# A task graph with list-scheduled engines, uncast hardware-queue loads, and the attention matmuls of two heads side by side in an attention and feed-forward kernel

## The chip, the cores and the metric

The kernel runs on one core of a Trainium2 chip. The metric is the device time of one execution in microseconds (us), lower is better. A profile is one execution; its span is some 2 us shorter than the time.

## The reference, cut to what matters

```python
# q, k, v: (8 batches, 8 heads, 576 tokens, 64), float32
scores = q @ k.T / sqrt(64);  scores = where(|i - j| <= 32, scores, -1e9)
attn = softmax(scores);       x = (attn @ v) as (8*576, 8*64)
# feed-forward: w_in (512, 2048), w_out (2048, 512)
h = x @ w_in;  g = s * relu(h)**2 + b;  out = g @ w_out        # (4608, 512) float32
```

The feed-forward is 9 blocks of 512 tokens. A block has a first stage, s1 (16 groups of 4 matmuls of 512 columns), and a second, s2 (4 groups of 16): 1152 matmuls in all. A block needs the attention of the one or two batches whose tokens it holds.

## The kernel before

A hand-written interleaving: between the steps of a head's attention one feed-forward item or transpose is put in. The GpSimd (POOL) queue loads q, k and v and casts them to bf16 on the way; q is transposed by DMA, k on TensorE; each head has its own matmuls, and its sums come from 64 columns of ones next to v.

```python
# loads: cast by the software queue, 256 B in, 128 B out
op("pool", lambda e: e.dma_start(
      dst[0:ns, blk, :].rearrange("p (h d) -> p h d", h=H),          # bf16 tile
      src[b, :, s0:s0 + ns, :].rearrange("h s d -> s h d")), ...)    # float32 in DRAM
# q by DMA transpose, 128 x 128 at a time
op("sp", lambda e: e.dma_start(QT[slot][:, pr, s0:s0 + ns],
      QPRE[slot][0:ns, blk, pr * 128:(pr + 1) * 128], transpose=True), ...)
# scores of one head: 64 rows of the array
op("pe", lambda e: e.matmul(SC[bank][0:nk, col:col + nq],
      lhsT=KT[slot][hb:hb + 64, pr, key0:key0 + nk],
      rhs=QT[slot][hb:hb + 64, pr, q0:q0 + nq], start=True, stop=True), ...)
# weighted sum and row sums of one head: [v | ones], 128 columns
op("pe", lambda e: e.matmul(AVACC[:, coff + rc0:coff + rc0 + nn],
      lhsT=VT[slot][0:nk, wi, h, vcol0:vcol0 + 128], rhs=et[0:nk, ecol:ecol + nn], ...), ...)
# ... 1/sum = exp(-ln(sum)) on ScalarE over 64 partitions, then XT = AVACC * (1/sum) on VectorE
# ... order of all engines: do_fill() between the steps, by hand
```

The softmax here doesn't subtract the row's maximum and nothing guards it: scores larger than these inputs give would overflow.

Of the kernel before, what the change touches and what calls it, by code (L numbers as in the profile page):

```python
# [17 lines left out]
NSBLK = (S + 127) // 128  # L18
# [4 lines left out]
class _Tok:  # L23

    __slots__ = ("sem", "val", "seq", "used")

    def __init__(self, sem, seq, val=None):
        self.sem = sem
        self.seq = seq
        self.val = val  # L30
        self.used = False


class _Op:
    __slots__ = ("stream", "fn", "sig", "amount", "tok", "eager")

    def __init__(self, stream, fn, sig, amount, tok, eager):
        self.stream = stream
        self.fn = fn
        self.sig = sig  # L40
        self.amount = amount
        self.tok = tok
        self.eager = eager


class _Wait:
    __slots__ = ("stream", "toks")

    def __init__(self, stream, toks):
        self.stream = stream  # L50
        self.toks = toks


class _Raw:
    __slots__ = ("stream", "fn")

    def __init__(self, stream, fn):
        self.stream = stream
        self.fn = fn


class _Sched:

    STREAMS = ("pe", "act", "dve", "pool", "sp")

    def __init__(self, sems):
        self.sem = sems
        self.seqctr = {k: 0 for k in sems}
        self.cnt = {k: 0 for k in sems}
        self.items = []  # L70
        self.clock = {k: {} for k in self.STREAMS}
        self.last_writer = {}
        self.readers = {}

    def _need(self, req, tok):
        if tok is None:
            return
        cur = req.get(tok.sem)
        if cur is None or tok.seq > cur.seq:
            req[tok.sem] = tok  # L80

    def _emit_waits(self, stream, req):
        clk = self.clock[stream]
        needed = []
        for sname, tok in req.items():
            c = clk.get(sname)
            if c is not None and c.seq >= tok.seq:
                continue
            clk[sname] = tok
            tok.used = True  # L90
            needed.append(tok)
        if needed:
            self.items.append(_Wait(stream, needed))

    def op(self, stream, fn, reads=(), writes=(), waits=(), accum=False, group=None):
        req = {}
        for w in waits:
            self._need(req, w)
        for r in reads:
            self._need(req, self.last_writer.get(r))  # L100
        for w in writes:
            if not accum:
                self._need(req, self.last_writer.get(w))
                for tok in self.readers.get(w, {}).values():
                    self._need(req, tok)
        if stream == "pe":
            req.pop("pe", None)
        self._emit_waits(stream, req)

        if group is not None:  # L110
            sig_name = group.sem
            amount = 16
            tok = group.final
            eager = True
            self.cnt[sig_name] += 16
        else:
            sig_name = stream
            amount = 1
            self.seqctr[sig_name] += 1
            tok = _Tok(sig_name, self.seqctr[sig_name])  # L120
            eager = False

        for r in reads:
            self.readers.setdefault(r, {})
            self._need(self.readers[r], tok)
        for w in writes:
            self.last_writer[w] = tok
            if not accum:
                self.readers[w] = {}
        self.items.append(_Op(stream, fn, sig_name, amount, tok, eager))  # L130
        return tok

    def raw(self, stream, fn):
        self.items.append(_Raw(stream, fn))

    def wait(self, stream, waits):
        req = {}
        for w in waits:
            self._need(req, w)
        self._emit_waits(stream, req)  # L140

    def dma_group(self, stream, names, rot, ndma):
        i = rot.setdefault("i", 0)
        name = names[i % len(names)]
        rot["i"] = i + 1
        prev = self.cnt[name]
        if prev > 0:
            self.wait(stream, [_Tok(name, self.seqctr[name], prev)])
        self.seqctr[name] += 1
        final = _Tok(name, self.seqctr[name], prev + 16 * ndma)  # L150

        class _G:
            pass

        g = _G()
        g.sem = name
        g.final = final
        return g

    def finalize(self):  # L160
        counts = {k: 0 for k in self.sem}
        streams = {k: [] for k in self.STREAMS}
        sems = self.sem
        for it in self.items:
            if isinstance(it, _Raw):
                streams[it.stream].append(it.fn)
            elif isinstance(it, _Wait):
                toks = it.toks

                def runw(eng, toks=toks):  # L170
                    for t in toks:
                        assert t.val is not None, "wait on an unassigned token"
                        eng.wait_ge(sems[t.sem], t.val)

                streams[it.stream].append(runw)
            else:
                do_inc = it.eager or it.tok.used
                if it.eager:
                    counts[it.sig] += it.amount
                elif do_inc:  # L180
                    counts[it.sig] += it.amount
                    it.tok.val = counts[it.sig]
                fn = it.fn
                sig = it.sig
                amount = it.amount

                if do_inc:
                    def runo(eng, fn=fn, sig=sig, amount=amount):
                        ins = fn(eng)
                        ins.then_inc(sems[sig], amount)  # L190
                else:
                    def runo(eng, fn=fn):
                        fn(eng)

                streams[it.stream].append(runo)
        self.streams = streams
        self.cnt_final = counts


def bass_sliding_window_symmetric__then__act_starrelu_kernel(  # L200
# [12 lines left out]
    NBLK_M = (T + 511) // 512  # L213

    with ExitStack() as es:
        _uid = {"n": 0}

        def sb(shape, dt, nm="t"):
            _uid["n"] += 1
            return es.enter_context(nc.sbuf_tensor(f"{nm}_{_uid['n']}", list(shape), dt))  # L220

        def ps(shape, dt=F32, nm="ps"):
            _uid["n"] += 1
            return es.enter_context(nc.psum_tensor(f"{nm}_{_uid['n']}", list(shape), dt))
# [4 lines left out]
        QPRE = [sb((128, NSBLK, DM), BF16, "qpre") for _ in range(2)]  # L229
        KPRE = [sb((128, NSBLK, DM), BF16, "kpre") for _ in range(2)]  # L230
        VT = [sb((128, NSBLK, H, 192), BF16, "vt") for _ in range(2)]
        QT = [sb((128, NPAIR, S), BF16, "qt") for _ in range(2)]
        KT = [sb((128, NPAIR, S), BF16, "kt") for _ in range(2)]
        EA = [sb((128, 352), BF16, "ea") for _ in range(2)]
        EB = [sb((128, 480), BF16, "eb") for _ in range(2)]
        RLN = [sb((128, S), F32, "rln") for _ in range(2)]
        RREC = [sb((128, S), F32, "rrec") for _ in range(2)]
        MA = sb((128, 352), BF16, "ma")
        MB = sb((128, 480), BF16, "mb")
        ONES_BF = sb((128, 192), BF16, "onesb")  # L240
        IDENT = sb((128, 128), BF16, "ident")
        ZERO_F = sb((128, 1), F32, "zero")
        GT = [sb((128, 16, 512), BF16, "gt") for _ in range(2)]
        R1 = [sb((128, 512), BF16, "r1") for _ in range(4)]
        OUTS = [sb((128, 512), F32, "outs") for _ in range(2)]
        CVEC128 = sb((128, 512), F32, "cvec128")
        CVEC_ROW = sb((1, 512), F32, "cvecrow")
        SB128 = sb((128, 2), F32, "sb128")
        SB_ROW = sb((1, 2), F32, "sbrow")
        ONES_ROW_F = sb((1, 128), F32, "ones_row_f")  # L250
        BCOL_BF = sb((128, 1), BF16, "bcol")

        SC = [ps((128, 512), F32, "sc") for _ in range(2)]
        TP = ps((128, 8, 128), BF16, "tp")
        AVACC = ps((128, 1024), F32, "avacc")
        HT = [ps((128, 512), F32, "ht") for _ in range(2)]
        OUTP = [ps((128, 512), F32, "outp")]

        dmaP = [f"dmaP{i}" for i in range(10)]
        dmaO = [f"dmaO{i}" for i in range(6)]  # L260
        dmaT = [f"dmaT{i}" for i in range(4)]
# [448 lines left out]
        def fill(n_items: int, batches_done: int):  # L710
            done = 0
            while done < n_items:
# [14 lines left out]
                if not progressed:  # L727
                    break
# [96 lines left out]
```

## Time and profile before

439.0 us, median of 3 runs (438.4 to 440.4).

The page gives busy tenths in 40 equal slices of the 437 us span (a digit is 10.9 us; 9 is 90% or more).

```profile
PE   0465459948998999899989989989998999999986
ACT  1064648971688677788788868777777333444300
DMA  3999999919610991494099165100000101011012
```

The first ten slices are thin on TensorE (PE) while the DMA engines are full: the kernel waits for its loads. The queues on the page say with what (packets, MB, share of the time of 16 DMA engines):

```profile
q0 software_dynamic: 115168, 18.36, 58.2%
q1 hardware_dynamic: 25792, 13.59, 12.3%
```

110,592 of the first are the 256-byte pieces of q, k, v, 33 ns each on average. The busy time of the engines in stretches (stretch, its length, then busy us and count of instructions by engine, granted TensorE clock as a share of full speed, DMA share, GB/s; the DMA share adds up the times of all packets, so it passes 1 where packets overlap on an engine):

```profile
core 0: us, PE busy (x) PEld busy (x) DVE busy (x) ACT busy (x) POOL busy (x), PEclk, DMA share, GB/s
40.00:90.00 50.00, 35.74 (x228) 17.15 (x231) 22.59 (x52) 35.85 (x57) 15.06 (x19) 1.00 1.49 144
90.00:140.00 50.00, 42.14 (x255) 18.87 (x259) 23.19 (x49) 31.16 (x48) 12.58 (x15) 0.90 0.68 60
140.00:190.00 50.00, 44.96 (x308) 21.42 (x313) 26.93 (x60) 37.60 (x60) 20.47 (x25) 1.00 1.01 88
190.00:240.00 50.00, 47.09 (x316) 22.17 (x322) 27.73 (x62) 39.83 (x62) 17.28 (x21) 1.00 1.12 95
240.00:290.00 50.00, 47.63 (x307) 22.07 (x312) 28.54 (x62) 39.23 (x62) 4.21 (x5) 1.00 0.35 58
```

From about 140 us TensorE is busy 45 to 48 us of every 50. A piece of the timeline at 123 us (start, duration, engine, line of the kernel, instruction and its count) shows what attention costs there; sc are scores, avacc weighted sums, ht and outp the feed-forward:

```profile
123.08 0.49 PE L475 MATMUL sc<-qt,kt 64*128 64x192 bf16 x3
123.50 1.04 PE L581 MATMUL ht<-xt,win 128*128 128x512 bf16 x4
124.38 0.32 PE L533 MATMUL avacc<-ea,vt 128*128 128x160 bf16 x3
124.53 0.48 PE L533 MATMUL avacc<-eb,vt 128*128 128x64 bf16 x6
125.17 0.81 PE L581 MATMUL ht<-xt,win 128*128 128x512 bf16 x3 [0.16 <-issue]
125.91 0.32 PE L475 MATMUL sc<-qt,kt 64*128 64x160 bf16 x2
126.17 1.90 PE L635 MATMUL outp<-wout,gt 128*128 128x512 bf16 x8
```

By start-to-start times a head's scores take 0.26 + 0.42 us and its weighted sum 0.57 us, so a batch of 8 heads about 10 us. From 337 us only the feed-forward is left, at 216 ns a matmul (8 in 1.73 us).

| | before |
|---|---|
| time, us | 438.7 |
| TensorE / ScalarE / VectorE busy, us | 371 / 262 / 204 |
| first s1 matmul, us | 57 |
| attention of a batch on TensorE, start to start | 10 us, plus 1.4 us of k transposes |

### The profile page before, as it was taken

What the parts mean: (1) busy time and instruction counts of PE and PEld (TensorE: products, weight loads), DVE (VectorE), ACT (ScalarE), POOL (GpSimd) and SP (SyncE); (2) the same over time, 40 slices, a digit from 0 to 9 for tenths busy, and PEclk for the clock granted to TensorE, in tenths of its full rate; (3) what the DMA queues carried; (4) which work ended last, traced back from release to release, by engine and by line L of the source; (5) the groups of instructions that cost most, each with busy time, mean ns of one, the idle gap of its engine ahead of it and who ended that gap; (6) DMA issues with size and microseconds to landing.
All of it is one profiled execution on the core that took longest, in us unless ns stands there. A gap on an engine that the chain in (4) does not pass through costs nothing.

```text
span 437.0 us, 6159 instructions
## 1 busy us (share of the span) xinstructions
PE 371.2 (85%) x2208; PEld 172.9 (40%) x2248; DVE 204.4 (47%) x430; ACT 262.1 (60%) x401; POOL 107.8 (25%) x140
## 2 busy tenths in 40 slices
PE   0465459948998999899989989989998999999986
PEld 0234224322443444444444434444443444444432
DVE  7444325543555464565555555544554333334321
ACT  1064648971688677788788868777777333444300
POOL 8998092019000830380092030000000000000000
PEclk9999999987999999999999999999999999999999
DMA  3999999919610991494099165100000101011012
GB/s 21 142 146 196 182 174 153 78 19 146 54 48 32 102 109 54 57 150 80 26 120 114 57 74 51 59 26 24 25 26 24 50 24 48 25 48 46 27 49 74
DMA packets 140990, 32.34 MB, mean 74 GB/s; under 512 B 133792, under 2 KB 135840, under 8 KB 140960
## 3 DMA queue, kind: packets, MB, share of 16 engines
q0 software_dynamic: 115168, 18.36, 58.2%
q1 hardware_dynamic: 25792, 13.59, 12.3%
q8 instruction: 18, 0.29, 0.3%
q14 instruction: 12, 0.10, 0.1%
HBM read 36.70 MB, written 9.44 MB: 106 GB/s over the span
## 4 chain that ended last, share of the span: by engine, by line
PE 72%; ACT 8%; POOL 7%; DMA 6%; issue 4%; DVE 3%; DVEq 0%; POOLq 0%; ACTq 0%
PE ht L581 26%; PE outp L621 15%; PE outp L635 14%; PE sc L475 8%; DMA kpre<-in_k_dram 6%; PE avacc L533 6%; ACT rln L545 3%; POOL kpre L372 2%; ACT rrec L552 2%; PE tp L421 2%; POOL vt L400 2%; POOL qpre L372 2%; DVE xt L558 2%; PE outp L348 1%; DVE outs L644 1%
## 5 line engine op out<-in xcount | busy, mean ns | idle before, releaser
L581 PE MATMUL ht<-xt,win 128*128 128x512 bf16 x550 | 143.9, 389 | 7.8 <-DVE xt L558 4.5
L558 DVE TENSOR_TENSOR xt<-avacc,rrec 64x576 bf16<-64x576 f32 x64 | 48.3, 755 | 95.0 <-ACT rrec L552 89.2
L581 PEld LDWEIGHTS ht<-xt,win 128*128 128x128 bf16 x576 | 49.1, 99 | 59.8 <-issue 6.8
L400 POOL DMA_DIRECT2D vt<-in_v_dram x40 | 34.0, 899 | 151.1 <-PE avacc L533 123.1
L621 PE MATMUL outp<-wout,gt 128*128 128x512 bf16 x279 | 67.0, 380 | 4.2 <-DVE outs L644 2.5
L635 PE MATMUL outp<-wout,gt 128*128 128x512 bf16 x283 | 68.8, 385 | 0.6 <-issue 0.5
L545 ACT ACTIVATE rln<-avacc,zero 64x576 f32<-64x576 f32 x64 | 47.0, 734 | 30.9 <-PE avacc L533 30.0
L488 ACT ACTIVATE eb<-sc,zero 128x480 bf16<-128x480 f32 x64 | 42.3, 661 | 26.1 <-PE sc L475 26.1
L475 PE MATMUL sc<-qt,kt 64*128 64x192 bf16 (+2 forms) x320 | 54.9, 258 | 1.0 <-DVE kt L431 0.4
L488 ACT ACTIVATE ea<-sc,zero 128x352 bf16<-128x352 f32 x64 | 35.2, 550 | 27.0 <-PE sc L475 26.7
L552 ACT ACTIVATE rrec<-rln,zero 64x576 f32<-64x576 f32 x64 | 49.4, 772 | 2.1
L475 PEld LDWEIGHTS sc<-qt,kt 64*128 64x128 bf16 (+1 forms) x320 | 22.3, 100 | 54.1 <-issue 29.1
L591 ACT ACTIVATE r_32<-ht,zero 128x512 bf16<-128x512 f32 x36 | 24.8, 688 | 28.6 <-PE ht L581 27.5
L533 PE MATMUL avacc<-ea,vt 128*128 128x160 bf16 (+2 forms) x192 | 22.0, 228 | 23.2 <-DVE xt L558 22.9
L591 ACT ACTIVATE r_30<-ht,zero 128x512 bf16<-128x512 f32 x36 | 24.7, 687 | 27.5 <-PE ht L581 26.5
L621 PEld LDWEIGHTS outp<-wout,gt 128*128 128x128 bf16 x288 | 26.1, 98 | 36.0 <-DVE outs L644 4.5
L635 PEld LDWEIGHTS outp<-wout,gt 128*128 128x128 bf16 x288 | 26.8, 99 | 31.7 <-issue 1.3
L372 POOL DMA_DIRECT2D kpre<-in_k_dram x40 | 38.0, 950 | 0.0
L372 POOL DMA_DIRECT2D qpre<-in_q_dram x40 | 37.8, 944 | 0.7 <-issue 0.7
L644 DVE SCALAR_TENSOR_TENSOR outs<-outp,sb_37,cvec_35 128x512 f32<-128x512 f32 x36 | 26.9, 748 | 22.4 <-PE outp L635 22.2
L495 DVE TENSOR_TENSOR eb<-eb,mb 128x480 bf16<-128x480 bf16 x64 | 26.0, 406 | 18.9 <-ACT eb L488 16.4
L533 PE MATMUL avacc<-eb,vt 128*128 128x64 bf16 (+3 forms) x384 | 33.2, 209 | 0.0
(45 smaller groups left out, 252.0 us busy)
## 6 DMA issues: line engine op xcount, KB each, us to landing
out_dram<-outs SPq DMA_DIRECT2D x36, 256.0 KB, 2.0
qpre<-in_q_dram POOLq DMA_DIRECT2D x32, 128.0 KB, 5.3
kpre<-in_k_dram POOLq DMA_DIRECT2D x32, 128.0 KB, 5.4
vt<-in_v_dram POOLq DMA_DIRECT2D x32, 128.0 KB, 4.8
qt<-qpre SPq DMA_TRANSPOSE x140, 4.9
win<-in_moe_w_in_dram POOLq DMA_DIRECT2D x1, 2048.0 KB, 15.6
wout<-in_moe_w_out_dram POOLq DMA_DIRECT2D x1, 2048.0 KB, 26.8
qpre<-in_q_dram POOLq DMA_DIRECT2D x8, 64.0 KB, 6.5
```

The source lines that it names most:

```text
L372: lambda e, src=src, dst=dst, s0=s0, ns=ns, blk=blk: e.dma_start(dst[0:ns, blk, :].rearrange("p (h d) -> p h d", h=H), src[b, :, s0:s0 + n ...
L400: lambda e, s0=s0, ns=ns, blk=blk: e.dma_start(VT[slot][0:ns, blk, :, 64:128], v[b, :, s0:s0 + ns, :].rearrange("h s d -> s h d"),),
L475: lambda e, key0=key0, nk=nk, q0=q0, nq=nq, col=col: e.matmul(SC[bank][0:nk, col:col + nq], lhsT=KT[slot][hb:hb + 64, pr, key0:key0 + nk], ...
L488: lambda e, ncols=ncols, et=et, prows=prows: e.activation(et[0:prows, 0:ncols], SC[bank][0:prows, 0:ncols], AF.Exp, bias=ZERO_F[0:prows, : ...
L533: stop=stop, coff=coff: e.matmul(AVACC[:, coff + rc0:coff + rc0 + nn], lhsT=VT[slot][0:nk, wi, h, vcol0:vcol0 + 128], rhs=et[0:nk, ecol:ec ...
L545: lambda e: e.activation(RLN[hp][srow0:srow0 + 64, :].rearrange("p (g c) -> p g c", g=2), acc2(srow0), AF.Ln, bias=ZERO_F[srow0:srow0 + 64 ...
L552: lambda e: e.activation(RREC[hp][orow0:orow0 + 64, :], RLN[hp][srow0:srow0 + 64, :], AF.Exp, bias=ZERO_F[srow0:srow0 + 64, :], scale=-1.0,),
L558: lambda e: e.tensor_tensor(XT[orow0:orow0 + 64, pr, t0:t0 + S].rearrange("p (g c) -> p g c", g=2), acc2(orow0), RREC[hp][orow0:orow0 + 64 ...
L581: lambda e, kc=kc: e.matmul(HT[hbank][:, 0:nt], lhsT=WIN_BF[:, kc, ft * 128:(ft + 1) * 128], rhs=XT[:, kc, t0:t0 + nt], start=(kc == 0), s ...
L591: lambda e: e.activation(R1[rslot][:, 0:nt], HT[hbank][:, 0:nt], AF.Relu, bias=ZERO_F[:, :], scale=1.0,),
L621: lambda e, fc=fc, obuf=obuf: e.matmul(OUTP[obuf][0:nr, :], lhsT=GT[gslot][:, fc, sub * 128:sub * 128 + nr], rhs=WOUT_BF[:, fc, :], start= ...
L635: lambda e, fc=fc, obuf=obuf: e.matmul(OUTP[obuf][0:nr, :], lhsT=GT[gslot][:, fc, sub * 128:sub * 128 + nr], rhs=WOUT_BF[:, fc, :], start= ...
```

## The change

The intent: (1) let a list scheduler order each engine's instructions from a graph of tasks with estimated costs, in place of the hand-made order; (2) load float32 by the hardware queues, without the slow cast, and cast on VectorE; (3) treat two heads at once: their score matmuls on rows 0-63 and 64-127 of the array, their sums on columns 0-63 and 64-127, so that both softmax activations use 128 partitions. Further, q and k of batches 2 to 7 are transposed by DMA, 128x512 at a time. A unit is half of the queries (320 or 256) of a pair of heads; a batch has 8.

```diff
+    def plan(self):                      # list scheduling: always the task that can start first
+                for t in open_[s]:
+                    c = (max(free[s], t.ready), t.key, t.n)
+            free[t.stream] = st + t.cost
+            if t.dma is not None:
+                dma_free = max(dma_free, st + 1300.0) + t.dma[1]
+                t.fin = dma_free + 700.0
... (the order so found is what each engine's program is)
-                    op("pool", lambda e, ...: e.dma_start(dst[0:ns, blk, :]..., src[b, ...]...))
+                lambda e: e.dma_start(STG[n][0:ns, blk, :].rearrange("p (h d) -> p h d", h=H), ...),
+                650.0, writes=[("STG", n, blk)], key=16 * (b - 2), waits=waits,
+                dma=("l" if stream == "sp" else "a", ns * 2048 / 290.0))
+            return add("dve", lambda e: e.tensor_copy(dst[0:ns, lo:hi, :], STG[n][0:ns, lo:hi, :]),
+                       150 + 267.0 * len(blks), ...)
+            add("sp", lambda e: e.dma_start(dst[:, :, s0:s0 + ns], NAT[n][0:ns, blk, :],
+                                            transpose=True), 1300.0, ..., dma=("t", 700.0), ...)
+            for (w, q0, nq) in PIECES[hf]:
+                for hh in range(2):       # two heads: two row tiles
+                    ... e.matmul(SC[:, hh, c0:c0 + nq],
+                        lhsT=KT[slot][64 * hh:64 * hh + 64, pr, 128 * w:128 * w + 128],
+                        rhs=QT[slot][64 * hh:64 * hh + 64, pr, q0:q0 + nq], start=True, stop=True)
+            for (dst, res) in ((SS, "SS"), (AV, "AV")):   # row sums, then weighted sum
+                ... e.matmul(dst[64 * hh:64 * hh + 64, ...], lhsT=lhs,      # two column tiles
+                             rhs=EX[e_][:, hh, c0:c0 + nq], ...)
+                    for n in "qkv":
+                        load(b, n, blk, waits=[wout[3]] if b == 1 else ())  # after the weights
... (hand-made interleaving, phase_A_steps, phase_B, fill and drain_moe removed)
```

The tile for the float32 data (STG) has one copy, and each engine runs its program strictly in the planned order.

## The prediction

> **What bounds it now.** Three stages, from the busy table by stretches and the timeline.
> (1) 0-116 us, fill. TensorE is busy 71 of 116 us, and slowly: the clock record has it at full rate only from about 70 us, and the ht matmuls at 57-66 us lie about 430 ns apart instead of 216. The chain of waits shows why: the POOL queue issues loads (0.88 us each), then 26 us of one load of k in flight while both weight matrices share the DMA engines (90% and more in the slices from 11 to 77 us). A casting 256 B packet takes 32-35 ns; a batch of q, k, v is 13,824 of them, 28 us of all 16 engines.
> (2) 116-337 us: TensorE saturated, 206 of 221 us busy. By start-to-start times one head costs 1.25 us (scores 0.26 + 0.42, weighted sum 0.57), a transposed block of k 0.28, eight 512-column matmuls 1.73-1.83. ScalarE is busy 171, VectorE 119: not the limit.
> (3) 337-437 us: feed-forward alone, 216 ns a matmul, at its floor.
>
> **What the change does.** The 1152 feed-forward matmuls x 216 ns = 249 us stay: the floor.
> - Two heads per matmul: 36 matmuls a pair of heads instead of 28. The Trainium skill ("TensorEngine Tiling (Array Packing)", Tiling Modes and Performance Considerations) gives up to 2x, but a change of mode drains the array, and column tiling loses fast weight load; no run yet shows either. Estimate from the times above: 0.75-1.2 us for a unit (half the queries of a pair of heads), 6-9.6 us a batch where 10 us stood; plus 1.4 us a batch of k transposes gone. Steady gain: 2-5 us a batch.
> - ScalarE: both softmax activations now use 128 partitions, so about 262 -> 228 us. VectorE: -28 us by the same filling, +43 us of casts (estimate: fp32 copies at two elements a cycle, "VectorE: DVE Perf Modes", perf-mode tier table; no fp32 SBUF copy is in the trace). About 200 us, off the path.
> - Loads without cast, on hardware queues, by data rate: I expect 18-25 ns a 256 B packet (the transposes' SBUF packets average 24), so a batch in 16-22 us instead of 28. Weights only after the first nine blocks, batch 1 after the weights. First feed-forward block near 32 us (was 57), but batch 1 lands near 65, so its attention ends and s1(1) starts near 75-80 us, against about 116 for steady work before. This is the larger gain, some 35 us.
>
> **Sum.** 78 + 8 blocks x 27.6 + 6 batches x 6-9.6 + 4 of tail = 339-360; with 3-4% of stalls, 358 us. Range 330-402. Faster by over 2%: 0.93; within 2%: 0.03; slower: 0.04.
>
> **What would show it.** First ht matmul near 30-35 us; DMA slices full until about 65 us; k/q/v packets under 25 ns; TensorE 90% busy from 80 us to the end; score and sum groups 0.3-0.4 us each start to start; VectorE wait on TensorE, not the reverse.
>
> **What would make it wrong.** A transpose of 128x512 may hold the SP queue several times the 1.23 us of today's 128x128: 60 of them at over 3.5 us would make SP the limit (400-450 us). Loads may not get faster than 33 ns a packet (+15-25 us). The two heads may not overlap (+20 us). The fixed order may stall TensorE where ScalarE runs late (+10-20 us).

## The result, and the profile after

The changed kernel is correct and takes 401.3 us, median of 4 runs (399.1 to 402.7), beside 438.7 us (437.7 to 440.4). The ratio is 0.912 (95% interval 0.908 to 0.916). Ratios here are the mean time of one kernel's runs over that of the other's of the same rounds, so not quite the ratio of the medians. Executions over 1.5% slower than the fastest of the same kernel are left out of the means. It is faster, but the time lies at the very top of my range of 330 to 402 us, one of the four runs above it, and the gain is 37 us where I had forecast 81.

The slices (10.0 us each) and queues of the changed kernel:

```profile
PE   0636988892996897789796969999999999999996
ACT  1547662653595387457464737677777764433310
DMA  8999999849968978967999542310000010010112
```

```profile
q1 hardware_dynamic: 141536, 43.40, 54.0%
q0 software_dynamic: 4288, 4.20, 6.4%
```

The start is better filled, and a 256-byte packet now takes 22 ns, but from 90 to 240 us TensorE has holes that were not there before. The same stretches:

```profile
core 0: us, PE busy (x) PEld busy (x) DVE busy (x) ACT busy (x) POOL busy (x), PEclk, DMA share, GB/s
40.00:90.00 50.00, 45.16 (x324) 19.71 (x327) 30.15 (x70) 26.51 (x41) 0.00 (x0) 0.93 0.92 168
90.00:140.00 50.00, 36.95 (x267) 16.04 (x269) 24.85 (x51) 27.36 (x45) 0.00 (x0) 0.86 1.06 188
140.00:190.00 50.00, 44.16 (x332) 19.42 (x336) 27.30 (x60) 33.65 (x54) 0.00 (x0) 0.93 0.85 165
190.00:240.00 50.00, 38.60 (x282) 17.23 (x286) 25.65 (x54) 26.33 (x41) 0.00 (x0) 0.93 0.86 175
240.00:290.00 50.00, 49.21 (x379) 21.86 (x385) 26.08 (x54) 36.70 (x58) 0.00 (x0) 1.00 0.17 48
```

Once the loads are over (the DMA share falls to 0.17) TensorE runs at 49 of 50 us. While they run, no engine is full. The waits say who waited for whom (total us, times, longest). The tiles stgq, stgk and stgv hold the float32 loads and natq, natk and vb their bf16 casts; sc are scores, ex their masked exponentials, ss the row sums, av the weighted sums:

```profile
DVE natq L375 <- DMA stgq<-in_q_dram: 44.0, 17, 8.9
PEld ss L453 <- DVE ex L441: 31.0, 16, 7.6
PE ss L453 <- DVE ex L441: 24.5, 8, 7.4
DVE natk L375 <- DMA stgk<-in_k_dram: 9.7, 8, 5.6
DVE vb L375 <- DMA stgv<-in_v_dram: 6.8, 8, 4.2
```

VectorE (DVE) stands 60.5 us in front of casts whose data has not landed, and TensorE stands for the masks (ex) that VectorE has not done. One such stall in the timeline, at 123 us (start, duration, engine, line, instruction; in brackets the idle time before it and what ended it):

```profile
123.20 0.56 DVE L441 TENSOR_TENSOR ex<-ex,mask 128x768 bf16<-128x768 bf16 x1 [0.71 <-ACT ex L438]
...
124.87 0.69 ACT L523 ACTIVATE r_31<-w,zero 128x512 bf16<-128x512 f32 x1
...
126.32 0.51 ACT L467 ACTIVATE rec<-lns,zero 128x256 f32<-128x256 f32 x1
...
129.70 0.69 DVE L375 CAST natq<-stgq 128x1024 bf16<-128x1024 f32 x1 [5.94 <-DMA stgq<-in_q_dram]
130.31 0.42 DVE L526 TENSOR_TENSOR gt<-r_30 128x512 bf16<-128x512 bf16 x1
130.64 0.42 DVE L470 TENSOR_TENSOR xt<-av,rec 128x256 bf16<-128x256 f32 x1
...
131.12 0.53 PE L453 MATMUL av<-ex,vb 128*64 128x96 bf16 x6 [4.37 <-DVE xt L470]
...
132.05 1.46 PE L534 MATMUL o<-wout,gt 128*128 128x512 bf16 x3 [0.41 <-DVE gt L526]
```

From 123.8 to 129.7 us VectorE does nothing: next in its program is a cast of the batch after the next, which waits for a load. The square (gt) and the division (xt) behind it had their inputs from ScalarE by 126.8 us, and TensorE waits for that xt for 4.4 us. After the stall the matmuls of L534 run at half rate (1.46 us for three). The windows view gives a granted clock of 0.57 from 128 to 136 us:

```profile
128.00:136.00 8.00, 4.48 (x17) 1.75 (x18) 4.41 (x9) 0.00 (x0) 0.00 (x0) 0.57 1.11 218
```

From 70 to 240 us it gives 0.92 on average; a clock that is either full or half (the trace has no other value) was then half for about 0.08 x 2 x 170 = 27 us of that stretch, which cost TensorE at most half of that, 14 us (an estimate). From 240 us it is 1.00. The Trainium skill ("TensorE: Matmul & The Clock Gate", Part 1) describes this, a clock that drops to half when the array idles for a window; this trace agrees: the clock fell during the stall of 4.4 us. The means of the whole span, 0.957 here and 0.984 before, are no witness: the clock's record begins only at 43 us here and at 70 us before, and the feed-forward matmuls just before that, about 430 ns apart, ran at half rate too.

The start of each feed-forward block (the first weight load of its s1, read from the trace) puts a size on it:

| us | s1(0) | s1(1) | s1(2) | s1(3) | s1(4) | s1(5) | s1(6) | s1(7) | s1(8) | span |
|---|---|---|---|---|---|---|---|---|---|---|
| changed kernel | 39 | 89 | 135 | 168 | 216 | 257 | 293 | 328 | 356 | 400.9 |

Where nothing is missing (from s1(5)) a block with attention takes 35-36 us, one without 27. Blocks 1 to 4 took 46, 33, 48 and 41.

### The profile page after: what moved, and what is told of

Same layout as the page of the kernel before. It is cut to its first block, busy times and chain, and to the rows that moved or that the text cites. A ratio compares the mean times of both kernels' runs of the same rounds, so it can differ in the third digit from the quotient of the medians.

```text
span 400.9 us, 6048 instructions
## 1 busy us (share of the span) xinstructions
PE 337.9 (84%) x2358; PEld 152.7 (38%) x2400; DVE 197.7 (49%) x415; ACT 219.4 (55%) x342; POOL 14.1 (4%) x40
## 4 chain that ended last, share of the span: by engine, by line
PE 50%; SPq 15%; DMA 8%; issue 2%; DVE 1%; ACT 1%; DVEq 0%
PE o L534 22%; PE w L517 21%; SPq L300 11%; DMA stgq<-in_q_dram 5%; SPq L383 4%; DMA stgv<-in_v_dram 3%; PE ss L453 3%; PE sc L429 2%; PE av L453 1%; SPq L549 1%; DVE ex L441 1%; ACT ex L438 0%; DVE outs L546 0%; ACT lns L464 0%; DVE gt L526 0%
## 5 line engine op out<-in xcount | busy, mean ns | idle before, releaser
L517 PE MATMUL w<-xt,win 128*128 128x512 bf16 x548 | 146.0, 392 | 4.3 <-issue 1.9
L534 PE MATMUL o<-wout,gt 128*128 128x512 bf16 x563 | 147.5, 389 | 2.0 <-issue 1.1
L517 PEld LDWEIGHTS w<-xt,win 128*128 128x128 bf16 x576 | 53.4, 100 | 68.1 <-issue 7.9
L534 PEld LDWEIGHTS o<-wout,gt 128*128 128x128 bf16 x576 | 52.6, 99 | 64.5 <-issue 5.0
L438 ACT ACTIVATE ex<-sc,zero 128x896 bf16<-128x896 f32 (+1 forms) x64 | 60.7, 949 | 9.5 <-PE sc L429 8.4
L464 ACT ACTIVATE lns<-ss,zero 128x320 f32<-128x320 f32 (+1 forms) x64 | 31.9, 499 | 50.7 <-PE ss L453 50.6
L441 DVE TENSOR_TENSOR ex<-ex,mask 128x896 bf16<-128x896 bf16 (+1 forms) x64 | 37.5, 588 | 23.0 <-ACT ex L438 22.8
L453 PE MATMUL ss<-ex,ones 128*64 128x96 bf16 (+2 forms) x384 | 25.8, 247 | 25.5 <-DVE ex L441 24.5
L523 ACT ACTIVATE r_28<-w,zero 128x512 bf16<-128x512 f32 x36 | 24.7, 687 | 27.3 <-PE w L517 26.1
L523 ACT ACTIVATE r_29<-w,zero 128x512 bf16<-128x512 f32 x36 | 24.7, 687 | 24.9 <-PE w L517 24.8
L523 ACT ACTIVATE r_31<-w,zero 128x512 bf16<-128x512 f32 x36 | 24.7, 687 | 21.7 <-PE w L517 21.7
L467 ACT ACTIVATE rec<-lns,zero 128x320 f32<-128x320 f32 (+1 forms) x64 | 34.2, 534 | 1.4
L523 ACT ACTIVATE r_30<-w,zero 128x512 bf16<-128x512 f32 x36 | 24.7, 686 | 15.9 <-PE w L517 14.7
L526 DVE TENSOR_TENSOR gt<-r_29 128x512 bf16<-128x512 bf16 x36 | 15.2, 423 | 22.6 <-ACT r_29 L523 22.3
L526 DVE TENSOR_TENSOR gt<-r_30 128x512 bf16<-128x512 bf16 x36 | 15.2, 423 | 19.1 <-ACT r_30 L523 19.0
L526 DVE TENSOR_TENSOR gt<-r_31 128x512 bf16<-128x512 bf16 x36 | 15.2, 422 | 18.4 <-ACT r_31 L523 18.3
```

Of the source, the lines that this page charges most:

```text
L438: add("act", lambda e: e.activation(EX[e_][:, :, 0:n], SC[:, :, 0:n], AF.Exp, bias=ZERO_F[:, :], scale=0.125), 280 + 2 * n * 0.834, reads= ...
L441: add("dve", lambda e: e.tensor_tensor(EX[e_][:, :, 0:n], EX[e_][:, :, 0:n], MASK[hf][:, :, :], ALU.mult), 170 + n / 0.96, reads=[("E", e_ ...
L453: fns.append(lambda e, q0=q0, nq=nq, hh=hh, c0=c0, i=i, dst=dst, lhs=lhs: e.matmul(dst[64 * hh:64 * hh + 64, q0 - u0:q0 - u0 + nq], lhsT=l ...
L464: add("act", lambda e: e.activation(LNS[e_][:, 0:nu], SS[:, 0:nu], AF.Ln, bias=ZERO_F[:, :], scale=1.0), 280 + nu * 0.834, reads=["SS", "Z ...
L467: add("act", lambda e: e.activation(REC[e_][:, 0:nu], LNS[e_][:, 0:nu], AF.Exp, bias=ZERO_F[:, :], scale=-1.0), 280 + nu * 0.834, reads=[( ...
L517: add("pe", [lambda e, kc=kc: e.matmul(W[wb][:, :], lhsT=WIN_BF[:, kc, ft * 128:(ft + 1) * 128], rhs=XT[:, kc, t0:t0 + TOK], start=(kc == ...
```

## The experiments

Theory 1: the fixed order is the fault. The plan believed in faster loads than there are, so it put casts on VectorE ahead of work that was ready, and an engine that runs in order can't go round them. Theory 2: the loads and transposes come too slowly whatever the order, either because they share one SP queue (2a) or because the DMA engines' packets are the limit (2b). A third suspicion concerned the two-heads matmuls. All kernels passed the comparison with the reference, even e4 and e13, whose results are wrong.

| | change to the changed kernel | us | ratio to before | s1(1) | s1(8) |
|---|---|---|---|---|---|
| changed kernel | | 401.3 | 0.912 | 89 | 356 |
| e1_plan_rates | plan told the measured load times | 376.9 | 0.857 | 100 | 331 |
| e12_plan2 | the same, for batches 1 to 7 only | 367.0 | 0.835 | 88 | 320 |
| e11_optimist | plan told still faster loads | 413.9 | 0.942 | 106 | 366 |
| e2_casts_pool | casts on GpSimd | 378.8 | 0.863 | 87 | 331 |
| e4_contig_loads | 2 KB packets (wrong data) | 355.7 | 0.809 | 81 | 309 |
| e5_loads_pool | loads from the GpSimd queue | 401.3, 402.1 | 0.914 | 106 | 365 |
| e6_head | e12, batch 1 before w_out | 366.3 | 0.833 | 83 | 319 |
| e7_head_pool | e6 + e2 | 364.4 | 0.829 | 81 | 317 |
| e8_cast_dma | casting loads, plan told so | 386.7 | 0.879 | 102 | 339 |
| e9_heads_serial | e1, one head after the other | 377.7 | 0.857 | 99 | 331 |
| e10_pe_transposes | e1, no DMA transposes | 389.7 | 0.886 | 99 | 342 |
| e13_same_rows | e1, both heads on the same rows | 388.6 | 0.884 | 100 | 340 |

(The last two columns are from the profiled execution; that of e5 was slow.)

### e1_plan_rates and e12_plan2: the same instructions in another order

```diff
-                650.0, ...            dma=(..., ns * 2048 / 290.0))
+                650.0 if b == 0 else 1140.0, ...  dma=("l", ns * 2048 / 230.0))
-                t.fin = dma_free + 700.0
+                t.fin = dma_free + (2500.0 if t.dma[0] in "lt" else 700.0)   # e12: only b > 0
```

> Same instructions as after, another order: the list scheduler is told what the trace shows (a load of 256 KB holds its queue 1.14 us and lands 2.5 us later than the rate gives; it assumed 0.65 us, 0.90 us and 0.7 us). Theory 1 (the fixed order puts a cast on VectorE before its load has landed, the masks, squares and divisions behind it wait, and TensorE with them): the 44 us that VectorE waits for loads of q falls below 15 us, TensorE's wait for the mask (31 us) falls too, blocks 1 to 4 take 35-38 us each, total 370-382 us. Theory 2 (the loads themselves, with the transposes on one SP queue, come too slowly for TensorE, whatever the order): total stays at 396-403 us and the wait moves to another instruction.

Measured: 376.9 us, 24 us less than the changed kernel. VectorE's waits for q are no longer in the list, those for k and v sum to 19 us, and the mask waits of TensorE fell from 31.0 and 24.5 us to 3.6 and 1.2. But its first batch came 10 us later (s1(1) at 100 us), since I had raised the landing time of the first batch's loads too, which are not late. e12 leaves the first batch as it was.

> The scheduler is told the measured load times for batches 1 to 7 only; the first batch is planned as in the changed kernel, weights in its order. Separates the two parts of e6. If the whole 30 us of slow blocks are the order's doing: s1 of block 1 at 86-92 us as in the changed kernel, blocks of 34-36 us, total 366-374 us, so that e6's other start is worth only 0-8 us. If e6's gain over e1 came from its other start: total 375-380 us as e1.

Measured: 367.0 us, 34 us less than the changed kernel, in the range expected of the order being the cause. s1(1) begins at 88 us as in the changed kernel, and from there to s1(8) it takes 232 us where the changed kernel took 267. The waits and the stretches of e12:

```profile
DVE natq L376 <- DMA stgq<-in_q_dram: 4.2, 3, 3.2
PEld ss L454 <- DVE ex L442: 8.3, 9, 4.5
PE ss L454 <- DVE ex L442: 5.3, 4, 4.2
```

```profile
40.00:90.00 50.00, 45.91 (x319) 20.29 (x318) 30.19 (x70) 26.64 (x41) 0.00 (x0) 0.90 0.97 168
90.00:140.00 50.00, 48.72 (x390) 21.75 (x389) 31.28 (x67) 39.36 (x65) 0.00 (x0) 1.00 1.01 182
140.00:190.00 50.00, 50.00 (x390) 21.91 (x388) 31.54 (x68) 35.48 (x58) 0.00 (x0) 1.00 0.82 167
190.00:240.00 50.00, 50.00 (x388) 22.46 (x387) 31.16 (x64) 35.72 (x57) 0.00 (x0) 1.00 0.95 184
```

Same loads, same packets (22.8 ns), same SP queue, and TensorE is busy 148.7 of the 150 us from 90 to 240 where it was busy 119.7. The granted clock is 1.00 there too. Theory 2 falls: for this stretch the delivery is fast enough. What follows is that the order cost 34 us, the half-rate matmuls after its stalls included. The new plan orders every engine anew, so e12 alone does not say that it was VectorE's order; for that stand the waits and e2 below.

### e11_optimist: the opposite dose

The plan gets 0.45 us, 450 B/ns and 0.5 us; nothing else changes.

> The opposite dose: the scheduler is told that loads are still faster (0.45 us to issue, 450 B/ns, landing 0.2 us sooner than assumed). Instructions and data as in the changed kernel. Theory 1 (casts placed before their loads land): the casts move earlier still, VectorE waits 55-90 us for loads, total 408-430 us. Rival (any reordering helps, e1's gain was luck): below 400 us.

Measured: 413.9 us, 13 us slower than the changed kernel, in the expected range, so it isn't so that any reshuffling helps. VectorE's waits for loads did not rise (38.1 us for q, 54.0 with k and v), though; 10.2 us of waits of casts for transposes came in their place (2.0 before), and TensorE's mask waits rose to 34.6 and 32.6 us. Part of the loss also moved forward: s1(1) begins at 106 us in place of 89, while blocks 1 to 4 take 161 us in all in place of 168. The total of a wait is not the cost: that depends on what stands behind it.

### e2_casts_pool: another cure for the same fault

```diff
-            return add("dve", lambda e: e.tensor_copy(...), 150 + 267.0 * len(blks), ...)
+            return add("dve" if b < 2 else "pool", lambda e: e.tensor_copy(...), ...)
```

> The casts of batches 2 to 7 go to the idle GpSimd; loads, transposes and all else stay. Theory 1 (casts that wait for loads block VectorE): VectorE no longer waits for loads, blocks 1 to 4 take 35-38 us, total 368-382 us even if a cast itself takes longer on GpSimd. Theory 2 (delivery of loads and transposes by SP is the limit): total 396-405 us.

Measured: 378.8 us, with the plan's belief in fast loads left as it was. The wait is still there, longer than ever, but on an engine that has nothing else to do:

```profile
POOL natq L376 <- DMA stgq<-in_q_dram: 148.1, 13, 44.7
```

A cast of 128x1024 takes GpSimd 1.09-1.15 us and VectorE 0.69 us; it does not matter. This is the clearest sign that not the lateness of the data but the engine that waits for it was the cost. (Its order on the other engines was planned anew as well, so it differs from the changed kernel by more than the casts.) It gets 22 of the 34 us; its block 1 still took 45 us. The trace has the rest in one place: VectorE waited 12.3 us, until 108 us, for an output to be stored, and TensorE 10.6 us for VectorE.

```profile
DVE outs L547 <- DMA out_dram<-outs: 14.4, 2, 12.3
```

The SP queue issued that store at 104.6 us, behind 14 loads that took it 15 us; the plan, still at 0.65 us a load, had counted 9. That reads as the same fault on another queue that runs in order; no run tested it.

### e4_contig_loads: what the loads' packets cost

```diff
-  src_of[n][b, :, blk * 128:blk * 128 + ns, :].rearrange("h s d -> s h d")
+  src_of[n][b].rearrange("h (a c) d -> (h a) (c d)", c=H)[blk * 128:blk * 128 + ns, :]
```

> Wrong result on purpose: each load of q, k, v takes as many bytes, but from contiguous rows of 2 KB instead of eight pieces of 256 B. Tests whether the loads' packets are the root, by taking most of their time away: a batch should come in about 8-9 us instead of 16. Theory 1 and theory 2 both expect most of the 40 us back, 355-372 us, from an earlier batch 1 (s1 of block 1 at about 80 us instead of 89) and from blocks 1 to 4 at 35 us. If it stays above 390 us, neither holds, and the SP queue's transposes or the engines' order without any late load are the cause.

Measured: 355.7 us. The data is wrong by construction; the comparison's tolerance does not see it. With the loads' bytes in packets of 2 KB (98 ns instead of 8 x 22) s1(1) begins at 81 us and block 1 takes 30 us; with the plan's numbers unchanged, VectorE's wait for q falls from 44.0 us to 3.4. This fits both theories; it says that pieces of 256 B are the root of the lateness, and that even with the order of e12, 11 us of the time (367.0 against 355.7) still hang on them, 8 of them before s1(1).

### e5_loads_pool: the loads on a queue of their own

Loads of batches 1 to 7 are issued from GpSimd (still uncast), transposes stay on SP.

> Loads of batches 1 to 7 are issued from the idle GpSimd queue instead of SP, so they no longer queue with the 13 us of transposes a batch; packets stay the same. Theory 2a (the SP queue, which alternates 16 us of loads with 13 us of transposes, is the limit): loads are issued earlier, total 365-385 us. Theory 2b (the DMA engines' packets are the limit): no change, 395-405 us. Theory 1: loads land earlier than the plan thought, so VectorE waits less: 370-390 us; the waits of VectorE for loads tell it from 2a, as they must fall with the time.

Measured: 401.3 and 402.1 us (two runs at 411.8 and 424.5 us were slow), the same as the changed kernel. So 2a's forecast fails. By itself it does not clear the queue, since the plan was again wrong, now about the transposes (waits of the profiled run, a slow one at 411.8 us):

```profile
DVE natq L375 <- DMA qt<-natq: 28.2, 4, 12.3
DVE natk L375 <- DMA kt<-natk: 19.0, 5, 8.3
```

VectorE's waits for loads fell to 16 us and 47 us of waits for transposes, which must have read the bf16 tile before the next cast writes it, took their place. That is theory 1 by another door, argued from these waits and not tested; e12 is what clears the queue. The packets did not stay the same, as I had expected: on this queue the trace records the loads of batches 1 to 7 in packets of 4096 B, 345 ns each. That is 21.6 ns per 256 B, so the DMA engines' time per byte hardly changed.

### e6_head and e7_head_pool: the start

```diff
-                        load(b, n, blk, waits=[wout[3]] if b == 1 else ())
+                        load(b, n, blk, waits=[win[3]] if b == 1 else ())   # w_out waits for these
```

> As e1_plan_rates (the scheduler told the measured load times, now for batches 1 to 7 only, as in e1 the first batch's attention came 10 us later than before), and the loads of batch 1 go out after the first weight matrix instead of after the second, which now waits for them. Theory (the rest of the gap to my prediction is the start: steady work began at 89 us, not 78, because SP stood still for 25.5 us until both weight matrices had landed): s1 of block 1 begins at 62-75 us, blocks of 34-36 us follow, total 342-360 us. Rival (the second weight matrix, coming later, holds back s2 of block 0 as long as batch 1 was held back): 368-378 us, as e1.

Measured: 366.3 us, as e12. s1(1) began 5 us earlier (83 us), not 15 to 25, and its two parts are settled by e12: the gain over e1 is the plan for the first batch, not the new order of loads. Blocks 1 and 2 took 33 and 34 us where e12 has 31 and 32, so most of the 5 us went again.

> e6 plus e2: measured load times, batch 1 before the second weight matrix, casts of batches 2 to 7 on GpSimd. If waits of VectorE for loads still cost something in e6, 355-362 us; if e6 is at TensorE's floor for its start (83 us + 8 blocks), no gain: 363-370 us.

Measured: 364.4 us, the best correct kernel, 37 us below the changed kernel and 74 below the kernel before. The casts on GpSimd are worth some 2 us here; once the plan is right the two cures do not add up.

### e8_cast_dma: undo the loads

Loads from the software queue, casting into double-buffered bf16 tiles; no casts on VectorE; the plan told of 126 B/ns.

> Undoes one part of the change: q, k, v are loaded by the software queue, which casts on the way, straight into bf16 tiles; no cast on VectorE. The scheduler is told the measured 32-35 ns a packet. Theory A (the way of loading matters because a casting packet takes 33 ns and not 22): with 28 us of loads and 6-8 us of transposes a batch the DMA engines need about as long as TensorE (34.5 us), and batch 1 lands 12 us later, so total 385-405 us against 377 in e1. Theory B (the way of loading does not matter once the order fits it, as VectorE has room): 370-382 us.

Measured: 386.7 us, 10 us above e1, theory A's range at its lower end. A packet took 32.5 ns instead of 22.7. Part of the difference is mine: TensorE waited 15.0 us at the start for the identity, which GpSimd made only after it had issued the loads, though s1(1) came just 3 us later than in e1. The granted clock was half for 31 us from 58 us on, against 10 us in e1, and by 120 us TensorE had started 20 feed-forward matmuls fewer. So in this pair of runs uncast loads are worth some 10 us or less, against the 35 us that I had put on the earlier start; the second copy of the bf16 tiles in e8 may hide a part, which was not tested.

### e9_heads_serial and e13_same_rows: do the two heads overlap?

In e9 the six score matmuls of a unit come as three of one head, then three of the other, and so for the sums.

> As e1, but within a unit all matmuls of the one head come before those of the other, so that no two neighbours lie on different rows or columns of the array; same count, same sizes. If the pairs overlap: score and sum groups grow from 0.28 us to 0.4-0.5 us start to start, a unit from 0.85 to 1.2-1.5 us, total 390-410 us. If they do not overlap (the gain comes from fewer transposes and fuller activations alone): total within 3 us of e1.

Measured: 377.7 us, as e1, and the groups take the same time. By my expectation that would mean no overlap, but the trace shows why it does not. Start times of one unit's score matmuls (us, columns; own reading of the trace, program order 160, 192, 96, 160, 192, 96):

```
273.596 160   273.606 160   273.676 192   273.686 192   273.758 96   273.768 96
```

TensorE started the second head's first matmul 10 ns after the first head's, ahead of two that come before it in the program. So TensorE finds the pairs itself, and not the build: e9's kernel, built again, has all matmuls of these groups in program order in TensorE's instruction stream. So e13 puts both heads on the same rows (a wrong result for every second head):

```diff
-                        lhsT=KT[slot][64 * hh:64 * hh + 64, pr, 128 * w:128 * w + 128],
-                        rhs=QT[slot][64 * hh:64 * hh + 64, pr, q0:q0 + nq],
+                        lhsT=KT[slot][0:64, pr, 128 * w:128 * w + 128],
+                        rhs=QT[slot][0:64, pr, q0:q0 + nq],
```

> Wrong result on purpose: as e1, but the score matmuls of both heads read partitions 0 to 63, so the pair lies on the same rows of the array and cannot overlap; sizes and counts as before. e9 did not settle the overlap, as TensorE ran the pairs side by side even from the serial order. If rows overlap: the group of six score matmuls grows from 0.29 us to 0.45-0.60 us start to start, 64 units x 0.15-0.3 = 10-20 us on TensorE, total 384-395 us. If not: 375-379 us.

Measured: 388.6 us, 11.7 us above e1. A group of scores takes 0.465 us start to start instead of 0.287, and 64 x 0.178 = 11.4 us, which is nearly the whole difference. The rows overlap. For the columns no run was made; but a group of row sums, 832 columns on average, took 0.209 us, and 832 columns at the feed-forward's 216 ns per 512 would take 0.351 us, so they must overlap too.

### e10_pe_transposes: undo the DMA transposes

> As e1, but q and k of all batches are transposed on TensorE (through the sum banks), none by DMA: SP loses 13 us a batch and the DMA engines 6-8. If delivery on SP still limits anything after the order is mended: 360-374 us. If TensorE is the limit: 10 blocks x 0.28 us x 6 batches = 17 us more on it and 25 us more on VectorE, so 385-398 us.

Measured: 389.7 us, 13 us above e1. A transposed block took TensorE 0.22 us (0.13 the last, half-sized one of a batch), so 60 of them take 12.2 us, nearly the whole loss: TensorE is the limit, and taking 13 us a batch off the SP queue bought nothing that shows. A second witness against 2a.

## Why the prediction was right or wrong

**Wrong: "Sum. 78 + 8 blocks x 27.6 + 6 batches x 6-9.6 + 4 of tail = 339-360; with 3-4% of stalls".** The failed step is the stalls. I counted 10 to 14 us for them and named, last on my list of risks, a fixed order that stalls TensorE "where ScalarE runs late". The order cost about 34 us (401.3 less e12's 367.0), and above all it was VectorE's order: casts placed by a plan that took a 256 KB load to occupy the DMA engines 0.90 us and to land 2.9 us after its issue, where the trace has 1.12 us between issues and some 5 us from issue to landing. The plan's rate makes 12 us of a batch's loads (3.54 MB at 290 B/ns); I expected 16-22 us, so I could have seen that the plan was too fast, and I still costed the loads as an amount of DMA time. What I did not ask is what a statically ordered engine does when a load is late. My own check, "VectorE wait on TensorE, not the reverse", is the one that the profile turned down.

**Wrong by 11 us: "s1(1) starts near 75-80 us".** It started at 89, and at 88 in e12. Batch 1's loads went out at 41.8 us and had landed by 61 us (I had said 65), and packets were as fast as I thought; its attention, from 58 to 88 us, took longer than the 10 to 15 us that I had left for it. Issuing the loads earlier (e6) moved it only to 83. Why it takes so long was not tested; ScalarE's share of a unit is (60.7 + 31.9 + 34.2) / 64 = 2.0 us, 16 us for the eight.

**Right in mechanism and size.**
- Packets of 18-25 ns: 22.2. A batch in 16-22 us: batch 1 was issued from 41.8 to 57.2 us, batch 2 to 75 us.
- A unit of attention at 0.75-1.2 us: 0.29 + 0.21 + 0.28 = 0.78 us start to start, so 6.2 us a batch where 10 us stood. I named the Trainium skill for "up to 2x" and a drain at each change of mode (the first stands in that page's Overview, not in the sections that I named; the loss of fast weight load under Restrictions); both are now measured. e13 shows the row overlap at 0.465 / 0.287 = 1.6. Between a feed-forward matmul's last column (reckoned at 216 ns per 512 columns) and the first score or sum matmul, and back, lie 95-99 ns, against 3 ns between feed-forward groups. Without the one such change that both groups of scores contain, the overlap is 0.370 / 0.192 = 1.9. Mostly a unit has four changes, 0.39 us; two of them lie in the feed-forward groups before, so a unit costs TensorE 0.78 + 0.19 = 0.97 us. The blocks agree: (35.3 - 27.4) / 8 = 0.99 us.
- ScalarE 228 us: 219. VectorE about 200: 198, though the casts in it took 50 us and not 43. A cast of 1024 elements took 0.69 us and one of 512 took 0.42 us; drawn on in a straight line to 2048 elements that is 1.24 us (an estimate), so my estimate from "VectorE: DVE Perf Modes" (perf-mode tier table: 1227 ns for an fp32 copy of 2048) holds.
- A DMA transpose of 128x512 holding SP several times 1.23 us: it did not happen, the median is 1.27 us.

**Off, without much weight.** First s1 matmul at 30-35 us: 39. "DMA slices full until about 65 us": with gaps, they stay busy to about 220 us, as the loads and transposes of a batch take the SP queue about 31 us of TensorE's 35.

**The headline.** With the order mended and nothing else (e12), the changed kernel takes 367.0 us, 9 us from the forecast of 358 and inside its range; what is left is about the size of the late s1(1). That the changed kernel itself still falls just inside the range is luck.

## What to carry to other kernels

A static schedule is as good as its durations: where engines run in order, one instruction placed ahead of its data holds up everything behind it, and the profile shows it as an engine that waits for a DMA while its neighbours wait for it and no engine is full. Feed the planner with times from the trace (interval between issues and time to landing, not bytes over bandwidth): loads planned still earlier cost 13 us (e11), and a first batch planned too late cost 10 us (e1 against e12). Or give work that waits for loads to an engine with nothing behind it, and look at the queue that it shares with others. And when you cost a rewrite, ask for each engine what stands behind the wait, not only whether the total fits.

## What the Trainium skill lacked or had wrong

- "TensorE: Matmul & The Clock Gate", Part 3, says that matmuls start and end strictly in program order. e9's trace differs: a matmul on the other half of the rows started 70 ns before two that precede it in the program (273.606 against 273.676 us for the first of them).
- "TensorEngine Tiling (Array Packing)", Key Properties, says that a change of mode drains the array but gives no cost: 95-99 ns per change here. Its note that column tiling disables fast weight load fits this trace: a load of 64 columns took 116-120 ns, one of 128 columns in plain mode 99-100.
- "DMA: Bandwidth & Descriptors" gives no time for which a DMA transpose holds its queue by shape on this chip: 1.23 us for 128x128 and 1.27 us for 128x512 here, so four times the data for about the same issue.
- The same page lists casts as a feature of the software queue without their price: 256 bytes of q, k, v take 32.5-33 ns with a cast to bf16, 22-23 ns uncast on the hardware queue, and 21.6 ns uncast on the software queue (e5, a slow run), so the price is the cast's and not the queue's.
- No page says how late a load lands behind others on its queue: about 5 us at the median for 256 KB, although the queue takes one every 1.1 us.
